# Long convolution and SwiGLU kernel: preceding block joined by a quarter turn after the product, third kernel spectrum built late, down projection with w_down stationary

## The chip, the core and the metric

The kernel runs on one core of one Trainium2 chip. A core has a matrix engine (PE, with its weight loads shown apart as PEld), a vector engine (DVE), an activation engine (ACT), a slower vector engine that also issues transfers (POOL), and a queue processor (SP) that only issues transfers. The metric is device time of one execution in microseconds: the median of 3 runs, 322.61 us before the change (322.45 to 322.96).

## What is computed

All tensors are bf16; the sequence has 2048 rows of 640 channels, the FFN is 1728 wide. `x` is `A_q`.

```python
def _A_ref(q, k, v, shift_k, ssm_k, ssm_D):       # q is layernorm(x)
    k_shift = sum over 4 taps t of k_pad[:, t:t+S] * shift_k[:, 3-t]
    kv = k_shift * v
    y = irfft(rfft(pad(kv)) * rfft(pad(ssm_k)))[:S]    # causal convolution, 2048 taps
    y = y + kv * ssm_D
    return q * y
def _B_ref(x, w_gate, w_up, w_down):
    return (silu(x @ w_gate) * (x @ w_up)) @ w_down
h = x + _A_ref(layernorm(x), A_k, A_v, A_shift_k, A_ssm_k, A_ssm_D)
h2 = h + _B_ref(layernorm(h), B_w_gate, B_w_up, B_w_down)
```

## The kernel before

The sequence is cut into 4 blocks of 512 rows (`NB = 4`, `MBLK = 512`). The convolution is done by blocks in a spectrum of odd frequencies: block `i` of `kv` becomes a spectrum X_i by matmuls with the constant `cs_t` (`x_transform`, L675); kernel block `p` becomes G_p by matmuls with `gb_t` (`g_transform0` L564, `g_transform` L612); products of X and kernel spectra are summed over pairs of blocks and brought back by matmuls with `ci_t` (`back`, L752). A spectrum is held as two "lanes" e = 0, 1 of 3 x 2 x 640 columns (two parts and a third, their half sum or sum, for complex products with three multiplications); one lane of 128 partitions has 0.98 MB.

A convolution of length 512 in this spectrum wraps: what runs over the block end comes back turned. The kernel before therefore joins each kernel block with the one ahead of it, once: `h_build` (L629 to L641) adds the neighbouring spectrum, turned by a quarter (parts swapped, one sign changed), to give H_p for p = 3, 2, 1. H_p goes to DRAM (`hd`) and comes back as lanes when a block needs it; X_i goes to DRAM (`xd`) likewise. `g_transform` for p = 1 to 3 works on folded kernel blocks (`g_fold`, L584 and L588: sum and difference of a block with its mirror image), which needs 4 or 6 matmuls a tile in place of 8; in the 6, two (L615) have a single row of `twos1` as weights. The time domain kernel blocks have time on the free axis, and are turned by DMA transposes (L542, L598).

Stages, by tag: C0 to C3 are the convolutions of the blocks, F0 to F3 the FFNs. A convolution stage: `shift` (taps on DVE, L653, L658, L659), `x_transform`, products (L937, L941 with earlier blocks; L955, L956 with H0; L895 in C0), `back` (L724, L732, L735 on DVE; L752 on PE; L410 on ACT; L758, L759 on DVE; `ln_stats` of h on ACT L700, L702, POOL L714), then the normed h (L767, called hn here) is turned by DMA transposes (L771) into `hlnT`. In F: gate and up projections (L831, 135 matmuls of 512 columns a block, weights streamed through 3 `wgu` buffers), silu and copy on ACT (L835, L836), product on DVE (L838), down projection with the activations `tT` as weights and `w_down` streaming (L856, 112 matmuls of 320 columns a block), with the residual h added on PE by an identity matmul (L852, 8 a block), copied out on ACT (L861).

No order is written by hand. Each piece of work is an `Op` with an engine, a duration, buffers and a priority; `Plan.schedule` walks a clock for each engine and picks, by priority and table offsets (`DELTA`, by tag, engine and function), which piece goes next. Buffers come from classes (`klass`) with a fixed number of slots, handed out first come first served. What comes out is one fixed order on each engine; SP issues its transfers strictly in that order, and one that must wait holds back all behind it.

The 4 PSUM tiles `ps` are shared by all matmul groups: PE fills one, ACT or DVE empties it, and only then is it free for another. `A_shift_k` is spread over partitions by 8 matmuls with `ones1` as weights at the very start (L511).

Of the kernel before, what the change touches and what calls it, by code (L numbers as in the profile page):

```python
# [54 lines left out]
    "C2 ACT back": 994,
    "C2 ACT evac": -900,
    "C2 ACT ln_stats": 97,
    "C2 DVE ln_stats": -1143,
    "C2 DVE shift": -33,
    "C2 DVE x_transform": -1000,  # L60
    "C2 PE x_transform": 30,
    "C2 SP k": 273,
    "C3 ACT evac": -103,
    "C3 ACT ln_stats": -100,
    "C3 DVE back": -1000,
    "C3 DVE ile_sequential_preLN__ssm_conv_h3__swiglu_ffn__prompt_kernel": -3,
    "C3 DVE ln_stats": -33,
    "C3 PE x_transform": -30,
    "C3 SP back": 200,
    "C3 SP k": 200,  # L70
    "C3 SP ldX": -1133,
    "C3 SP v": -1027,
    "C3 SP x": -30,
    "F0 PE ffn": 2872,
    "F0 POOL o": 200,
    "F0 SP w": 30,
    "F1 ACT ffn": 73,
    "F1 POOL o": 300,
    "F2 POOL o": -327,
    "F2 SP w": 100,  # L80
    "F3 DVE ffn": 30,
    "F3 SP w": 1030,
    "G ACT evac": 1662,
}
OPT = (True, (0, 1, 2, 3), (0,), (0, 1, 2, 3))
# [6 lines left out]
def make_consts():  # L92
# [24 lines left out]
    for n, (b, odd) in enumerate(((me, True), (pe, False), (po, True), (mo, False))):  # L117
        full = np.concatenate([np.full((HALF, 1), 2.0 * odd), (-1.0) ** odd * b[:, :0:-1], b], 1)
        for tt in range(NS):
            gb[:, tt, n, :] = full[:, tt * P:(tt + 1) * P].T  # L120
# [33 lines left out]
class Op:  # L154
    __slots__ = ("i", "eng", "dur", "fn", "deps", "succ", "allocs", "frees", "pri", "nwait", "ready", "soft", "alts", "key", "start", "end", "tag", "nbytes")


class Plan:
# [25 lines left out]
    def op(self, eng, dur, fn, r=(), w=(), pri=None, nbytes=0, alloc=(), alt=(), name=None):  # L184
        o = Op()
        o.i, o.eng, o.dur, o.fn, o.nbytes = len(self.ops), eng, dur, fn, nbytes
        o.alts = [(eng, dur, fn)] + list(alt)
        o.pri = self.pri if pri is None else pri
# [16 lines left out]
    def schedule(self):  # L205
# [37 lines left out]
        while done < len(ops):  # L243
# [40 lines left out]
            if o.nbytes:  # L284
                fly = flight[o.eng != "POOL"]
                s = max(st + o.dur + self.DMA_FIX, dma_free)
# [33 lines left out]
def kernel(  # L320
# [48 lines left out]
    NLANE, NWK, NS25, NWG = 7, 6, 3, 3  # L369
    klass("lane", NLANE, (P, 3, 2, D))  # L370
    klass("wk", NWK, (P, NS, D))
    klass("s25", NS25, (P, 2, D))
    klass("o", 2, (P, 2, D))
# [87 lines left out]
    taprows = [B("o", f"taps{k}") for k in range(2)]  # L461

    class Row:


        def __init__(self, k):
            self.b, self.k, self.dep = taprows[k // 2], k % 2, (taprows[k // 2], 1 << (k % 2))

        @property
        def t(self):  # L470
            return self.b.t[0:1, self.k, :]

# [17 lines left out]
    HB = 990  # L490


    def setup():
# [7 lines left out]
        with pl.at(-9.2):  # L501
            dma(lambda: ident.t[:], lambda: id_h.ap(), 32 * KB, w=[ident], q="ACT")
            pl.op("ACT", 0.46, lambda: nc.scalar.dma_start(out=skip.t, in_=A_ssm_D.rearrange("(o d) -> o d", o=1)), w=[skip.dep], nbytes=8 * KB, name="skip")
        for b, v in ((ones1, 1.0), (twos1, 2.0), (mhalf, -0.5)):
            dve(0.08, lambda b=b, v=v: nc.vector.memset(b.t[:], v), [], [b])
# [34 lines left out]
    def g_load0():  # L540
# [8 lines left out]
    def g_transform0(gT):  # L549

        def row():
            return gv(gT)[0:1, 0, :]
        dve(0.41, lambda: nc.vector.tensor_add(tap[0].t, skip.t, row()), [gT, skip.dep], [tap[0].dep])
        dve(0.41, lambda: nc.vector.tensor_sub(tap[1].t, skip.t, row()), [gT, skip.dep], [tap[1].dep])
        for b in (1, 3, 0, 2):
            tp = tap[1 - b % 2]
            for c in range(2):
                ps = B("ps")

                def mm(ps=ps, b=b, c=c, tp=tp):  # L560
                    for h in range(2):
                        hs = slice(h * NH, (h + 1) * NH)
                        for tt in range(NS):
                            nc.tensor.matmul(ps.t[:, h, 0:NH], gb_t.t[:, tt, b, c * P:(c + 1) * P], gv(gT)[:, tt, hs],  # L564
                                             start=(tt == 0), stop=False)
                        nc.tensor.matmul(ps.t[:, h, 0:NH], ones1.t[:], tp.t[:, hs], start=False, stop=True)  # L566
                pe(10 * c_mm(320), mm, [(gb_t, 2 - b % 2), gT, ones1, tp.dep], [ps])
                evac_lane(ps, H0, b, c)

    def g_fold(p):  # L570


        gst = B("h", f"gst{p}")

        def g():
            return flat(gst.t[:]).rearrange("p (c t) -> p c t", c=NDC)
        dma(g, lambda: A_ssm_k[:, p * MBLK:(p + 1) * MBLK].rearrange("(c p) t -> p c t", p=P), FULL, w=[gst])
# [5 lines left out]
        def sums():  # L583
            nc.vector.tensor_add(v()[:, :, 0], g()[:, :, HALF:MBLK], g()[:, :, HALF:0:-1])  # L584
            nc.vector.tensor_copy(v()[:, :, 0, 0:1], g()[:, :, HALF:HALF + 1])

        def diffs():
            nc.vector.tensor_sub(v()[:, :, 1], g()[:, :, HALF:MBLK], g()[:, :, HALF:0:-1])  # L588
            if p == 1:
                nc.vector.tensor_copy(s0c[p].t[:], g()[:, :, 0:1])  # L590
            else:
                nc.vector.tensor_add(s0c[p].t[:], s0c[p - 1].t[:], g()[:, :, 0:1])
            nc.vector.tensor_copy(v()[:, :, 1, 0:1], s0c[p].t[:])
        dve(c_tt(2 * D) + 0.25, sums, [gst], [(gf, 1)])
        dve(c_tt(2 * D) + 0.4, diffs, [gst] + ([s0c[p - 1]] if p > 1 else []), [(gf, 2), s0c[p]])
        gT = B("wgu", f"gT{p}")
        for dc in range(NDC):
            pl.op("SP", 1.25, lambda dc=dc: nc.sync.dma_start_transpose(out=gv(gT)[:, :, dc * P:(dc + 1) * P], in_=v()[:, dc].rearrange("p n t -> p (n t)")),  # L598
                  [gf], [(gT, 1 << dc)], nbytes=256 * KB, name="gT")
        return gT  # L600

    def g_transform(p, gT, dst):
        for b in (1, 3, 0, 2):
            e, n = b // 2, 1 - b % 2
            for c in range(2):
                ps = B("ps")

                def mm(ps=ps, b=b, c=c, n=n):
                    for h in range(2):
                        hs = slice(h * NH, (h + 1) * NH)  # L610
                        for tt in range(2):
                            nc.tensor.matmul(ps.t[:, h, 0:NH], gb_t.t[:, 2 + tt, b, c * P:(c + 1) * P], gv(gT)[:, 2 * n + tt, hs],  # L612
                                             start=(tt == 0), stop=(tt == 1 and n == 0))
                        if n:
                            nc.tensor.matmul(ps.t[:, h, 0:NH], twos1.t[:], gv(gT)[0:1, 2, hs], start=False, stop=True)  # L615
                pe((6 if n else 4) * c_mm(320), mm, [gb_t, gT] + ([twos1] if n else []), [ps], alloc=[dst[e].b])
                evac_lane(ps, dst, b, c)

    def g_sum_dve():
        for e in range(2):  # L620
            dve(c_tt(2 * D), lambda e=e: nc.vector.tensor_add(H0[e].t[:, 2], H0[e].t[:, 0], H0[e].t[:, 1]), [H0[e](15)], [H0[e](48)])
# [251 lines left out]
    with pl.at(-9):  # L873
        gT0 = g_load0()
# [123 lines left out]
```

## Time and profile before

| | us |
|---|---|
| median of 3 runs | 322.61 |
| the profiled execution's own time | 322.3 |
| its span, first to last instruction | 320.5 |
| PE busy | 283.2 (88%) |
| DVE busy | 222.6 (69%) |
| ACT busy | 192.7 (60%) |
| POOL busy | 32.2 (10%) |
| DMA moved | 67.52 MB, 211 GB/s mean |

The span is cut into stages below. A line of the timeline gives the start, how long the merged row lasts, engine, source line, operation, what is written from what, how often, and in brackets how long the engine stood idle ahead of it and what ended that. A row of groups gives count, then busy time and the mean duration of one in ns.

### The profile page before, as it was taken

The page shows a single profiled execution, that of the slowest core. Times are in us where ns is not written, and L with a number is a line of the kernel's source. Part 1 is how long each engine was busy: PE and PEld are TensorE (multiplying, and loading weights), DVE is VectorE, ACT ScalarE, POOL GpSimd, SP SyncE. Part 2 cuts the span into 40 slices and gives each one's busy share as a digit, 9 for nine tenths or more (in the row PEclk, how much of TensorE's full clock was granted, in tenths as well). Part 3 has the DMA queues.
Part 4 walks back from the last instruction along what each step waited for, and adds up shares of the span by engine and source line. Part 5 has one row for each costly group of instructions (what it writes and reads, how often), then busy time and mean ns, then how long its engine had stood idle before and what let it go on. Part 6 is the DMA issues. An engine that isn't in the chain of part 4 may idle for free.

```text
span 320.5 us, 4107 instructions
## 1 busy us (share of the span) xinstructions
PE 283.2 (88%) x1484; PEld 143.2 (45%) x1484; DVE 222.6 (69%) x284; ACT 192.7 (60%) x359; POOL 32.2 (10%) x34
## 2 busy tenths in 40 slices
PE   1499949983998859989989999999999999999993
PEld 0133622450254315555534545665444665444662
DVE  2992399479677999999999999986999730222100
ACT  1121895879399942594689768155995573445310
POOL 0000003003011140023002001300011020000000
PEclk9999995897599959999999999999999999999998
DMA  8998049436959999999965999999656224560011
GB/s 164 285 361 264 2 82 352 120 89 171 244 209 338 399 418 265 398 390 187 334 223 166 351 272 353 198 338 399 154 111 170 63 49 117 152 154 2 0 41 41
DMA packets 75911, 67.52 MB, mean 211 GB/s; under 512 B 33842, under 2 KB 70259, under 8 KB 75381
## 3 DMA queue, kind: packets, MB, share of 16 engines
q1 hardware_dynamic: 73662, 54.77, 59.0%
q0 software_dynamic: 2080, 12.45, 10.0%
q8 instruction: 11, 0.18, 0.2%
q10 hardware_dynamic: 150, 0.04, 0.1%
q14 instruction: 8, 0.07, 0.1%
HBM read 49.56 MB, written 12.45 MB: 193 GB/s over the span
## 4 chain that ended last, share of the span: by engine, by line
PE 25%; issue 22%; DVE 18%; ACT 17%; DMA 10%; SPq 3%; POOL 3%; POOLq 0%; DVEq 0%; ACTq 0%
PE ps L831 5%; PE ps L612 5%; DMA wgu<-in_B_w_gate_dram 5%; PE ps L564 4%; ACT junk L700 4%; ACT junk L702 3%; DVE lane L937 3%; PE ps L752 3%; DMA lane<-xd 3%; POOL mv L714 3%; PE ps L615 2%; PE ps L675 2%; DVE wk L653 2%; SPq L542 2%; ACT sg L835 2%
## 5 line engine op out<-in xcount | busy, mean ns | idle before, releaser
L831 PE MATMUL ps<-hlnT,wgu 128*128 128x512 bf16 x540 | 122.6, 384 | 8.4 <-DMA wgu<-in_B_w_gate_dram 4.8
L831 PEld LDWEIGHTS <-wgu 128*128 128x128 bf16 x540 | 53.0, 99 | 75.4 <-issue 11.0
L835 ACT ACTIVATE sg<-ps 128x512 bf16<-128x512 f32 (+1 forms) x56 | 33.5, 599 | 38.2 <-PE ps L831 36.0
L856 PE MATMUL ps<-wdA,tT 128*128 128x320 bf16 x384 | 55.6, 299 | 0.0
L856 PEld LDWEIGHTS <-tT 128*128 128x128 bf16 (+1 forms) x448 | 42.2, 98 | 20.6 <-issue 4.8
L838 DVE TENSOR_TENSOR tT<-sg,uc 128x512 bf16<-128x512 bf16 (+1 forms) x56 | 23.3, 420 | 35.7 <-ACT uc L836 35.4
L714 POOL TENSOR_TENSOR mv<-mv,mhalf 128x2 f32<-128x2 f32 (+1 forms) x12 | 21.9, 1827 | 183.2 <-DVE mv L712 183.2
L836 ACT CAST uc<-ps 128x512 bf16<-128x512 f32 (+1 forms) x56 | 32.8, 585 | 2.1 <-DVE tT L838 1.3
L861 ACT CAST o<-ps 128x640 bf16<-128x640 f32 x16 | 11.0, 691 | 35.1 <-PE ps L856 35.1
L612 PE MATMUL ps<-wgu,gb_t 128*128 128x320 bf16 x96 | 23.1, 370 | 10.0 <-ACT wdA L408 5.0
L937 DVE TENSOR_TENSOR lane<-lane,lane 128x3840 bf16<-128x3840 bf16 x12 | 25.8, 2154 | 4.5 <-DMA lane<-xd 4.5
L653 DVE TENSOR_TENSOR wk<-krun,w 128x2560 bf16<-128x2560 bf16 (+1 forms) x20 | 23.8, 1215 | 0.0
L408 ACT CAST lane<-ps 128x640 bf16<-128x640 f32 x31 | 20.0, 708 | 5.0 <-PE ps L615 4.5
L675 PE MATMUL ps<-wk,cs_t 128*128 128x320 bf16 x128 | 21.5, 332 | 0.8 <-ACT wdA L408 0.8
L564 PE MATMUL ps<-wgu,gb_t 128*128 128x320 bf16 x64 | 17.8, 425 | 4.4 <-DMA gb_t<-const_gb 4.4
L658 DVE TENSOR_TENSOR wk<-wk,wk 128x2560 bf16<-128x2560 bf16 (+1 forms) x15 | 18.1, 1213 | 0.0
L410 ACT ACTIVATE s<-ps,mv 128x640 bf16<-128x640 f32 x16 | 12.7, 795 | 7.8 <-PE ps L752 5.4
L675 PEld LDWEIGHTS <-cs_t 128*128 128x128 bf16 x128 | 13.5, 107 | 8.7 <-issue 1.6
L612 PEld LDWEIGHTS <-gb_t 128*128 128x128 bf16 x96 | 8.5, 107 | 18.4 <-issue 14.4
L408 ACT CAST h<-ps 128x640 bf16<-128x640 f32 x7 | 4.9, 699 | 19.0 <-PE ps L566 19.0
L752 PEld LDWEIGHTS <-ci_t 128*128 128x128 bf16 x128 | 12.4, 98 | 6.3 <-issue 1.0
L738 ACT ACTIVATE h<-wk,mv 128x640 bf16<-128x640 bf16 x16 | 13.4, 839 | 0.0
(83 smaller groups left out, 314.2 us busy)
## 6 DMA issues: line engine op xcount, KB each, us to landing
lane<-hd SPq DMA_DIRECT2D x10, 960.0 KB, 7.4
wgu<-in_B_w_gate_dram SPq DMA_DIRECT2D x24, 320.0 KB, 4.7
wgu<-in_B_w_up_dram SPq DMA_DIRECT2D x24, 320.0 KB, 4.4
lane<-xd SPq DMA_DIRECT2D x6, 960.0 KB, 7.4
xd<-lane POOLq DMA_DIRECT2D x4, 960.0 KB, 8.6
hd<-lane POOLq DMA_DIRECT2D x4, 960.0 KB, 9.1
krun<-in_A_k_dram SPq DMA_DIRECT2D x3, 1120.0 KB, 8.2
wk<-in_A_v_dram SPq DMA_DIRECT2D x4, 640.0 KB, 6.5
```

The source lines that it names most:

```text
L408: nc.scalar.copy(dst(), src())
L564: nc.tensor.matmul(ps.t[:, h, 0:NH], gb_t.t[:, tt, b, c * P:(c + 1) * P], gv(gT)[:, tt, hs], start=(tt == 0), stop=False)
L612: nc.tensor.matmul(ps.t[:, h, 0:NH], gb_t.t[:, 2 + tt, b, c * P:(c + 1) * P], gv(gT)[:, 2 * n + tt, hs], start=(tt == 0), stop=(tt == 1 an ...
L653: nc.vector.tensor_mul(dst.t[:, sl, :], ks, w4.t[:, j:j + 1, :].broadcast_to([P, n, D]))
L675: nc.tensor.matmul(ps.t[:, h, 0:NH], cs_t.t[:, s, n, c * P:(c + 1) * P], kv.t[:, s, h * NH:(h + 1) * NH], start=(a == 0), stop=(a == 1))
L714: pl.op("POOL", 1.4, lambda: nc.gpsimd.tensor_tensor(c(NS), c(2 * NS), mhalf.t[:, 0:len(slots)], op=ALU.pow), [(mv, bits << 8), mhalf], [( ...
L831: nc.tensor.matmul(ps.t[:, k, :], wg.t[:, kt, off:off + P], hT.t[:, kt, :], start=(kt == 0), stop=(kt == NDC - 1))
L835: act(c_act(MBLK) + 0.02, lambda ps=ps, sg=sg, np_=np_: nc.scalar.activation(sg.t[0:np_, :], ps.t[0:np_, 0, :], ACT.Silu), [(ps, 1)], [sg])
L836: act(c_act(MBLK), lambda ps=ps, uc=uc, np_=np_, lo=up_lo, k=len(offs) - 1: nc.scalar.copy(uc.t[0:np_, :], ps.t[lo:lo + np_, k, :]), [(ps, ...
L838: dve(c_tt(MBLK), lambda sg=sg, uc=uc, c=c, np_=np_: nc.vector.tensor_mul(tv()[0:np_, c, :], sg.t[0:np_, :], uc.t[0:np_, :]), [sg, uc], [( ...
L856: nc.tensor.matmul(ps.t[:, hh, 0:NH], tv()[0:np_, c, m * P:(m + 1) * P], wdc(c)[0:np_, hh * NH:(hh + 1) * NH], start=(c == 0 and not oadd) ...
L937: dve(c_tt(6 * D), lambda xl=xl, hl=hl: nc.vector.tensor_mul(xl.t[:], xl.t[:], hl.t[:]), [xl(), hl()], [xl()])
```

## The change

It has three named parts and several that come with them.

1. **Quarter turn after the product.** `h_build` is gone. The kernel spectra G_p are used as they are (their third part by `g_sum`). In `back`, the two combinations of the lanes (now buffers of a new class `eo`, r = 0 the sum, r = 1 the difference) of the block before are kept, and the new block's are added to them with parts swapped and one sign changed (L703 of the changed kernel). So block i needs only X_j times G_(i-j), and the neighbour comes from the kept `eo`.
2. **Third spectrum late.** G_3 is built in C3 (`g_block(3)`) and not at the start; it never goes to DRAM. G_1 and G_2 go to DRAM, and are used straight from their lanes when their block first needs them.
3. **Down projection turned** (`DSWAP`, blocks 0 to 2): w_down is the weight operand, `tT` streams; 5 x 14 matmuls of 512 columns a block (L803). The result is channel-major (`yT`, in a `wgu` buffer), is turned back by 5 DMA transposes a block (L514), and the residual is added on DVE (L811). Block 3 keeps the old form, with the residual on PE.
4. Only kernel block 3 is folded (`FOLD = (3,)`); blocks 1 and 2 take 8 matmuls a tile, none with a single row. Block 0 is loaded plainly and turned by 20 PE transposes (L525), not by a DMA transpose; its tiles still have one single-row matmul (`skip`) behind each 4.
5. Buffers: lanes 7 to 6, `wk` 6 to 5, `s25` 3 to 2, the two `o` halves become one whole, `eo` 3 new. Products with H0 in C1 and C2 are done in thirds (L931, L932). `DELTA` is a new table.

```diff
-OPT = (True, (0, 1, 2, 3), (0,), (0, 1, 2, 3))
+OPT = (True, (3,), (0,), (3,), (0, 1, 2))
...
-    NLANE, NWK, NS25, NWG = 7, 6, 3, 3
+    NLANE, NWK, NEO, NS25, NWG = 6, 5, 3, 2, 3
...
-        pl.op("SP", 2.5, lambda: nc.sync.dma_start_transpose(out=gv(gT), in_=A_ssm_k[:, 0:MBLK]), [], [gT], nbytes=FULL, name="gT")
+                        nc.tensor.transpose(pt[:, tt, dc * P:(dc + 1) * P], gsv(gst)[:, dc, (2 * a + tt) * P:(2 * a + tt + 1) * P], ident.t[:])
...
+                        if fold:
+                            ks = [(gb_t.t[:, 2 + tt, b, cs], gv(gT)[:, 2 * (1 - b % 2) + tt, hs]) for tt in range(2)]
...
+                        else:
+                            ks = [(gb_t.t[:, tt, b, cs], gv(gT)[:, tt, hs]) for tt in range(NS)]
+                            if p == 0:
+                                ks.append((ones1.t[:], skip.t[0:1, 0, hs]))
...
-            def f(e=e):
-                nc.vector.tensor_add(hp[e].t[:, 0], hp[e].t[:, 0], hm[e].t[:, 1])
-            def g(e=e):
-                nc.vector.tensor_sub(hp[e].t[:, 1], hp[e].t[:, 1], hm[e].t[:, 0])
...
+            old = before[r]
+            if old is not None:
+                for n in range(2):
+                    m = 3 << (2 * n)
+                    dve(c_tt(2 * D), lambda n=n, x=x, old=old, v=v: getattr(nc.vector, ("tensor_sub", "tensor_add")[n])(v(old)[:, 1 - n], v(x)[:, n], v(old)[:, 1 - n]),
+                        [(x, m), (old, 15 - m)], [(old, 15 - m)])
+            src.append((x, (0, 1)) if old is None else (old, (1, 0)))
+            before[r] = x
...
+        if i in DSWAP:
+            yT = B("wgu", f"yT{i}")
+            o = B("o", f"o{i}")
...
+                                nc.tensor.matmul(ps.t[:, 0, :], wdc(c)[0:np_, dc * P:(dc + 1) * P], tv()[0:np_, c, :], start=(c == 0), stop=(c == 13))
...
+                    tr_dma(lambda dc=dc: o.t[:, :, dc * P:(dc + 1) * P], lambda dc=dc: yT.t[:, dc, :], [(yT, 1 << dc)], [(o, 1 << dc)], alloc=[o], name="yT")
```

6. On SP at the start, the transfer of `gb_t` (the constant of the kernel spectra) has moved behind v, `cs_t`, `ci_t` and two pieces of w_down, and no transpose stands ahead of any of them any more.

**The order, place one: PE at the first X transform.** In the kernel before (`wgu_88` is the turned kernel block 0, `o_84` holds the single rows, `wk_75` is the kv of block 0) six tiles of kernel spectrum 0 stand ahead of it and two behind:

```order
L564 LDWEIGHTS gb_t
L564 MATMUL ps_65<-wgu_88,gb_t 128x320
L566 LDWEIGHTS ones_113
L566 MATMUL ps_65<-o_84,ones_113 128x320
L675 LDWEIGHTS cs_t
L675 MATMUL ps_66<-wk_75,cs_t 128x320
```

Changed (`wgu_87` is the turned kernel block 0, `wk_74` the kv):

```order
L582 LDWEIGHTS gb_t
L582 MATMUL ps_65<-wgu_87,gb_t 128x320
L582 LDWEIGHTS ones_108
L582 MATMUL ps_65<-o_83,ones_108 128x320
L638 LDWEIGHTS cs_t
L638 MATMUL ps_66<-wk_74,cs_t 128x320
```

The rows read alike; what moved is that here one tile stands ahead and seven behind.

**Place two: SP in C3.** Before (`xd`, `hd` are X and kernel lanes in DRAM, `hlnT` is the turned hn of block 2, `wk_75` is x):

```order
L771 DMA_TRANSPOSE hlnT_95<-s_0_80 128x5x128 x2
L430 DMA lane_67<-xd_120 128x3840
L430 DMA lane_70<-hd_126 128x3840
L430 DMA lane_68<-xd_122 128x3840
L430 DMA lane_72<-hd_124 128x3840
L430 DMA wk_75<-in_A_q_dram 128x2560
```

Changed (`wgu_88` holds yT of block 1 in the transposes, and weights in the last row):

```order
L409 DMA lane_72<-xd_114 128x3840
L514 DMA_TRANSPOSE hlnT_94<-s_0_81 128x5x128 x2
L409 DMA lane_71<-hd_120 128x3840
L514 DMA_TRANSPOSE o_83<-wgu_88 128x4x128 x2
L409 DMA lane_70<-xd_116 128x3840
L409 DMA lane_69<-hd_118 128x3840
L409 DMA wgu_88<-in_B_w_gate_dram 128x5x256
```

The transposes of o have come between the lane loads; eight lanes are loaded in C3 where ten were, with 6 slots for lanes in place of 7, and slots 71 and 72 are filled again as soon as a product has emptied them.

**Place three: DVE at the end of C3.** Before (`wk_74` and `lane_69` are what `back` reads):

```order
L956 TENSOR_TENSOR lane_67<-lane_67,lane_71 128x3840
L838 TENSOR_TENSOR tT_91<-sg_96,uc_98 128x512
L724 TENSOR_TENSOR lane_67<-lane_67 128x2560
L732 TENSOR_TENSOR wk_74<-lane_69,lane_67 128x1280 x2
L735 TENSOR_TENSOR lane_69<-lane_69,lane_67 128x1280 x2
```

Changed (`eo_79` is what r = 0 reads, `eo_80` what r = 1 reads):

```order
L698 TENSOR_TENSOR eo_78<-lane_67,lane_72 128x1280 x2
L703 TENSOR_TENSOR eo_79<-eo_78,eo_79 128x1280 x2
L791 TENSOR_TENSOR tT_90<-sg_95,uc_98 128x512
L698 TENSOR_TENSOR eo_78<-lane_67,lane_72 128x1280 x2
L703 TENSOR_TENSOR eo_80<-eo_78,eo_80 128x1280 x2
```

Four instructions stand where two did for each r: the turned sums have come into the last block's chain.

More of the change, by code (lines that the diff above doesn't have):

```diff
@@ L67 @@
[L67 to L83, printed above, removed]
+    "C0 ACT back": 3601,
+    "C0 ACT evac": -1548,
+    "C0 ACT g_sum": 1997,
+    "C0 DVE g_sum": -3262,
@@ L547, in evac_lane, with g_fold @@
         evac(D, lambda: v2(dst[e].t[:, n, c, :]), lambda: r3(ps.t), [ps], [dst[e](1 << (2 * n + c))], EITHER_G)
[L549 to L577, printed above, removed]
+    def g_fold(p, gst):
         gf = B("wk", f"gf{p}")
@@ L605, in g_transform, with mm @@
             for c in range(2):
                 ps = B("ps")
-                def mm(ps=ps, b=b, c=c, n=n):
+                def mm(ps=ps, b=b, c=c):
+                    cs = slice(c * P, (c + 1) * P)
                     for h in range(2):
                         hs = slice(h * NH, (h + 1) * NH)
[L611 to L615, printed above, removed]
@@ new lines, in g_block @@
+    def g_block(p):
+        if p in FOLD and p - 1 not in FOLD:
+            pl.op("POOL", 0.5, lambda: nc.gpsimd.memset(gb_t.t[0:1, 2, 0::2, :], 1.0), [], [(gb_t, 1 << k) for k in range(2)], name="first")
+        pm[p] = [Lane(B("lane", f"H{p}{e}")) for e in range(2)]
+        gst = g_load(p)
+        gT = g_turn_dma(p, g_fold(p, gst) if p in FOLD else gst)
+        g_transform(p, gT, p in FOLD)
+        g_sum(p)
+        if p < NB - 1:
+            for e in range(2):
+                dma(lambda e=e: HDR[p, e].t[:], lambda e=e: pm[p][e].t[:], LANE_B, r=[pm[p][e]()], w=[HDR[p, e]], q="POOL")
```

300 lines of the change are left out of this document (149 added, 151 removed).

## The prediction

> **What bounds the kernel now.** I read the busy shares first, then the span cut into stages, then the timelines of DVE and PE where stages meet.
>
> ```profile
> PE 283.2 (88%) x1484; PEld 143.2 (45%) x1484; DVE 222.6 (69%) x284; ACT 192.7 (60%) x359; POOL 32.2 (10%) x34
> ...
> PEclk9999995897599959999999999999999999999998
> ```
>
> By shares PE is the bound. The stages say more (columns: length, then busy time and count of PE, PEld, DVE, ACT, POOL; granted clock, DMA share, GB/s):
>
> ```profile
> 0.00:13.40 13.40, 2.42 (x8) 0.91 (x8) 6.89 (x13) 2.67 (x3) 0.20 (x4) 1.00 0.93 197
> 13.40:35.00 21.60, 21.52 (x71) 7.97 (x72) 13.20 (x23) 5.38 (x8) 0.00 (x0) 1.00 0.87 276
> 35.00:77.00 42.00, 32.11 (x170) 15.67 (x169) 31.29 (x42) 34.95 (x66) 4.68 (x4) 0.87 0.48 142
> 77.00:98.00 21.00, 18.97 (x76) 7.62 (x76) 13.90 (x22) 14.41 (x22) 2.13 (x4) 0.70 0.78 236
> 98.00:204.40 106.40, 97.75 (x531) 51.19 (x531) 103.45 (x121) 75.15 (x150) 17.62 (x14) 0.97 0.95 306
> 204.40:268.90 64.50, 63.97 (x377) 35.59 (x374) 47.91 (x54) 41.59 (x82) 5.92 (x6) 1.00 0.63 185
> 268.90:320.50 51.60, 46.51 (x256) 24.29 (x255) 5.95 (x14) 18.60 (x33) 1.63 (x3) 0.98 0.25 67
> ```
>
> From 98 to 204 DVE is full (103.45 of 106.40) and PE is not (97.75). Up to 98 nothing is full for long: chains over PE, ACT and DVE, with the PE clock down. The last 51.6 are PE alone. Three rows cut the span where it can be added up: the end of hn of block 0, the end of what `back` of block 3 needs, and the start of F3.
>
> ```profile
> 79.40 0.80 DVE L767 TENSOR_SCALAR s<-h,mv 128x640 bf16<-128x640 bf16 x2
> ...
> 249.17 1.55 DVE L735 TENSOR_TENSOR lane<-lane,lane 128x1280 bf16<-128x1280 bf16 x2
> ...
> 268.91 29.31 PE L831 MATMUL ps<-hlnT,wgu 128*128 128x512 bf16 x135
> ```
>
> So the span is 80.2 (to hn0) + 170.5 (DVE's long stretch, to 250.7) + 18.2 (to F3) + 51.6 (F3) = 320.5. I work out the four terms for the changed kernel. The execution's own time, 322.3, is 1.8 above its span, and the median of the runs 0.3 above that.
>
> **Term 1, up to hn0.** PE at the start:
>
> ```profile
> 13.48 1.25 PE L564 MATMUL ps<-wgu,gb_t 128*128 128x320 bf16 x4 [4.44 <-DMA gb_t<-const_gb]
> ...
> 31.74 0.44 PE L566 MATMUL ps<-o,ones 1*128 1x320 bf16 x1
> 32.12 5.97 PE L675 MATMUL ps<-wk,cs_t 128*128 128x320 bf16 x32
> 37.94 0.70 PE L564 MATMUL ps<-wgu,gb_t 128*128 128x320 bf16 x4
> ...
> 41.23 0.30 PE L566 MATMUL ps<-o,ones 1*128 1x320 bf16 x1
> ...
> 77.07 0.69 PE L612 MATMUL ps<-wgu,gb_t 128*128 128x320 bf16 x2 [5.00 <-ACT wdA L408]
> ```
>
> From 13.48 to 32.12 twelve groups of five take 1.55 each. Behind the X transform four of them take 0.90 each (37.94 to 41.53). The granted clock reads 1.00 in both (0.00 to 35.00 above), yet the pace differs by 1.7; so that column does not show what held the start back. In this mixture with single-row matmuls the slow pace held 18.6 us, and it ended inside the X transform, which has none.
>
> The X transform needs kv, which DVE makes:
>
> ```profile
> 9.25 2.29 DVE L653 TENSOR_TENSOR wk<-krun,w 128x1280 bf16<-128x1280 bf16 x3
> ...
> 21.19 0.83 DVE L659 TENSOR_TENSOR wk<-wk,wk 128x1280 bf16<-128x1280 bf16 x1
> ```
>
> The two tap rows (0.8 us inside this stretch) are gone, and the half for r = 0 is done two instructions (1.5) before the end: the X transform, now second on PE, starts at 22.0 - 0.8 - 1.5 = 19.7, and not at 32.1. It takes 6 as before, warming PE: 25.7. The seven tiles left are 14 groups: 14 x 0.90 = 12.6, to 38.3, against 41.5. That `gb_t` lands later costs nothing: its 13.48 moves by a few us, and only one tile (3.1) waits for it ahead of 19.7.
>
> From there ACT leads:
>
> ```profile
> 36.58 2.50 ACT L408 CAST lane<-ps 128x640 bf16<-128x640 f32 x4
> 38.92 1.32 ACT L622 ACTIVATE h<-h 128x1280 bf16<-128x1280 bf16 x1
> ...
> 41.58 0.74 ACT L702 ACTIVATE junk<-wk 128x640 bf16<-128x640 bf16 x1
> ...
> 42.44 0.74 ACT L700 ACTIVATE junk<-wk 128x640 bf16<-128x640 bf16 x1
> ...
> 64.65 0.80 ACT L410 ACTIVATE s<-ps,mv 128x640 bf16<-128x640 f32 x1 [0.56 <-PE ps L752]
> ...
> L738 ACT ACTIVATE h<-wk,mv 128x640 bf16<-128x640 bf16 x16 | 13.4, 839 | 0.0
> ...
> L714 POOL TENSOR_TENSOR mv<-mv,mhalf 128x2 f32<-128x2 f32 x8 | 12.0, 1496 | 92.2 <-DVE mv L712 92.2
> ```
>
> A copy costs 0.6, a statistic 0.86 from start to start. After 38.3: last copy (39.5), two statistics (41.3), two scalings (43.9), then the changed order has 9 copies and 3 h rows ahead of the first result of `back` (9 x 0.6 + 3 x 0.84 = 7.9, to 51.8), four results with a scaling and a copy between (4 x 0.8 + 1.3 + 0.6 + about 0.9 of waiting for PE = 6, to 57.8), and 8 statistics (6.9, to 64.7). Then 0.4 of small sums, the first two hn (0.8), a product on DVE of 2.15 beside the power's 1.5, the last two hn (0.8) and about 1 of signals: **70.0**. Before, it took 38.7 from the end of G0; here 31.7, since `back` no longer stands behind single-row tiles at the slow pace and G3 is not built here at all (the 77.07 row is its wait). Term 1: 80.2 to 70.0.
>
> **Term 2, DVE to the end of block 3's products.** The idle time in the old 170.5:
>
> ```profile
> L838 DVE TENSOR_TENSOR tT<-sg,uc 128x512 bf16<-128x512 bf16 (+1 forms) x28 | 11.6, 419 | 4.8 <-ACT uc L836 4.5
> ...
> 214.02 2.16 DVE L937 TENSOR_TENSOR lane<-lane,lane 128x3840 bf16<-128x3840 bf16 x1 [1.20 <-DMA lane<-xd]
> 219.50 2.16 DVE L937 TENSOR_TENSOR lane<-lane,lane 128x3840 bf16<-128x3840 bf16 x1 [3.32 <-DMA lane<-xd]
> ```
>
> 4.8 between 98 and 204, 4.5 for lanes, 6.5 ahead of 98 (21.0 less 13.9, a little of it before hn0), 0.6 besides: 16.4, so 154.1 of work. Removed after hn0: `h_build`, 18 instructions of 1280 (0.75 each by L735's pair) and 2 scalings, 14.5; one tap product and two lane products that now come earlier (1.4 + 4.2). Added ahead of block 3's end: 12 quarter-turn sums (9.0), four sums of the last `ps` of 1280 and two scalings (4.0), the fold of block 3 (1.9), 4 residual sums (3.0), and 1.4 since the thirds (24 x 0.75) take more than 8 whole ones (2.08 each); 0.9 less by products of F2 that move behind the end. That is -20.1 + 19.3 - 0.9 = -1.7: **the quarter turn saves DVE nothing**, it moves the work. Idle time in the new order: DVE reaches X1's sums about 5 after hn0, while ACT has six copies of G2, a scaling and eight copies of X1 behind 64.7 (14 x 0.6 + 1.3, to 74.4), and PE, idle for some 4 ahead of them, begins them slowly as at 77.07 (2.5): 77, a wait of 3. FFN products: 5 as now. Residual sums waiting for five transposes: 1. Lanes:
>
> ```profile
> L430 SPq DMA_DIRECT2D lane<-hd x10: 319/338/558, 126.3 to 212.8; - x10
> L430 SPq DMA_DIRECT2D lane<-xd x6: 319/369/796, 127.3 to 210.7; - x6
> ...
> DMA to landing us min/median/max: 5.2/7.4/10.5
> ```
>
> With 6 slots, slot 72 is refilled once its product is done and is needed 5.6 of DVE work later, slot 71 3.7 later, slot 70 4.7 later. Landing at 5.2 gives waits of 0, 1.5 and 0.5, at 7.4 they are 2, 3.7 and 2.7, at 10.5 about 17 in all with the others. I take 5, between the first two, since two reloads can overlap. Sum: 154.1 - 1.7 + 14 = **166.4**.
>
> **Terms 3 and 4.** From the last DVE input, PE needs `back` for r = 1 (2.3) and the down projection that is left, 63 matmuls of 512 columns at 29.31/135 = 0.217: 2.3 + 13.7 = 16.0, plus 0.1 of signalling. hn3 and its transposes take about as long: 262.78 + 0.80 - 251.78 = 11.8 from `back` to hn3 before, some 1 less now as r = 0 is further ahead, then a second transpose (1.2) and a landing (3.1).
>
> ```profile
> 251.78 2.33 PE L752 MATMUL ps<-lane,ci_t 128*128 128x320 bf16 x16
> ...
> 262.78 0.80 DVE L767 TENSOR_SCALAR s<-h,mv 128x640 bf16<-128x640 bf16 x2 [0.88 <-POOL mv L714]
> ...
> 311.42 3.42 PE L856 MATMUL ps<-wdA,tT 128*128 128x320 bf16 x24
> 314.68 0.81 PE L856 MATMUL ps<-wdB,tT 128*128 128x320 bf16 x4
> ...
> L771 SPq DMA_TRANSPOSE hlnT<-s x16: 1200/1227/2444, 77.8 to 264.5; - x16
> ...
> DMA to landing us min/median/max: 2.6/3.1/7.0
> ```
>
> Term 3: **16.1**. F3 is unchanged in form: **51.6**. As to PE, a narrow matmul costs (314.68 - 311.42)/24 = 0.136, so the turned down projection saves 120 x 0.136 - 70 x 0.217 = 1.1 a block, and G3 adds 32 x 0.136 = 4.4: its work from F0 on is the same within 1. F0 starts near 77 and waits some 3.5 for the first silu; up to `back` of block 3 stand three gate and up projections (88), 2.1 down projections (32) and 7 transforms of 32 (24), with some 4 of gaps: 228.5, 8 before DVE's 236.4. So what PE saves is covered by DVE, and where PE falls more than 8 behind, that cover is gone (rival 3).
>
> Sum: 70.0 + 166.4 + 16.1 + 51.6 = 304.1, with 1.8 and 0.3: **306**.
>
> **Rivals.**
> 1. *The single-row mixture cools PE again.* Seven tiles then cost 3.10 and not 1.80: 7 x 1.30 = 9.1, and everything behind shifts: 315. For it: the mixture never warmed PE in 18.6 us. Against: it ran warm for 3.6 us here, and rows that start cold (77.07) follow an idle gap of 5. The Trainium skill ("TensorE: Matmul & The Clock Gate", Part 1) says the gate opens after about 3.4 us of sustained activity and closes after an idle window; by it G0 stays warm, as I forecast. The row from 13.48 to 32.12 contradicts its first half, since activity without a gap stayed slow five such windows long. So: 14 in 100.
> 2. *Waits shrink.* Lanes land at 5.2, X1 is ready in time, ACT's chain is 3 shorter: 3 + 6 less, 297. 9 in 100.
> 3. *SP holds everything (slower than before).* In C3 the lane loads, the transposes of hn and o, and F2's weights stand in one SP order; o's transposes wait for PE's down projection, lanes behind them for the transposes, DVE for the lanes, FFN products for weights behind the lanes. If each load lands in 10.5, waits are 17 in place of 5 (+12), and the weights come late as they did once before:
>
> ```profile
> 116.15 6.60 PE L831 MATMUL ps<-hlnT,wgu 128*128 128x512 bf16 x20 [4.80 <-DMA wgu<-in_B_w_gate_dram]
> ```
>
> 4.8, and 2.3 for ten matmuls at the slow pace (6.60 less 20 x 0.217): +7. 306 + 19 = 325. It decides once PE is more than the 8 late. Against it: DMA moves two lanes less in C3. 10 in 100.
> 4. *Two half losses together*, 319 to 323: 7 in 100.
>
> **How the numbers follow.** Forecast 60 in 100 (301 to 312). The range reaches over rival 1 and most of rival 2: 298 to 319; outside are rival 3, rival 4 and a little below. A measurement of this kernel can tell 0.2% (0.65 us) from no change. Faster: 60 + 14 + 9 + 4 = 87; within 0.2%: 3; slower: 10.
>
> **What would show it.** Right: the X transform starts near 20, hn0 ends near 70, DVE is full from there with lane waits of some 5, `back` of block 3 gets its last input near 236, F3 takes 51.6. Wrong: G0's groups at 1.55 behind the X transform; PE, not DVE, the fuller engine from 80 to 230; SP waiting for o's transposes while DVE waits for lanes.

## The result and the profile after

The changed kernel takes 311.25 us (median of 4 runs, 309.74 to 314.09), the kernel before 322.78 (322.45 to 323.24): a ratio of 0.965, 95% interval [0.958, 0.973]. The forecast was 306. The profiled execution of the changed kernel took 310.19 with a span of 308.3, against a forecast span of 304.1. Comparisons leave disturbed runs out, so a ratio is not always the quotient of the medians beside it.

Busy shares and the granted clock of the changed kernel (share of the span in brackets, then instructions; below, the clock in 40 slices):

```profile
PE 267.4 (87%) x1394; PEld 134.5 (44%) x1394; DVE 224.5 (73%) x294; ACT 192.8 (63%) x362; POOL 28.2 (9%) x33
...
PEclk9999999979999999999999999899999999999999
```

PE is 16 us shorter in busy time. In the kernel before, the slices of 8.0 us with a low clock lay from 48 to 64 (5 and 8), from 72 to 88 (7 and 5) and at 112 (5), the last slice left aside; now there are two, a 7 at 62 and an 8 at 193 (slices of 7.7). The three rows that cut the span, now (start, us, engine, line):

```profile
67.92 0.79 DVE L737 TENSOR_SCALAR s<-h,mv 128x640 bf16<-128x640 bf16 x2
...
235.77 1.55 DVE L703 TENSOR_TENSOR eo<-eo,eo 128x1280 bf16<-128x1280 bf16 x2
...
256.24 29.38 PE L784 MATMUL ps<-hlnT,wgu 128*128 128x512 bf16 x135
```

| Term | before | forecast | measured |
|---|---|---|---|
| 1, to the end of hn of block 0 | 80.2 | 70.0 | 68.7 |
| 2, to the end of what block 3's `back` needs | 170.5 | 166.4 | 168.6 |
| 3, to F3 | 18.2 | 16.1 | 18.9 |
| 4, F3 | 51.6 | 51.6 | 52.1 |

All of the gain is in term 1: -11.5. The other three together are 0.7 shorter than before (239.6 after 240.3), where 6.2 was forecast.

PE at the start, timeline of the changed kernel:

```profile
18.04 1.25 PE L582 MATMUL ps<-wgu,gb_t 128*128 128x320 bf16 x4 [4.64 <-DMA gb_t<-const_gb]
...
21.15 5.80 PE L638 MATMUL ps<-wk,cs_t 128*128 128x320 bf16 x32
26.80 0.70 PE L582 MATMUL ps<-wgu,gb_t 128*128 128x320 bf16 x4
27.43 0.30 PE L582 MATMUL ps<-o,ones 1*128 1x320 bf16 x1
...
39.20 4.52 PE L582 MATMUL ps<-wgu,gb_t 128*128 128x320 bf16 x32
...
50.83 4.52 PE L723 MATMUL ps<-eo,ci_t 128*128 128x320 bf16 x32
```

The X transform starts at 21.15 (32.12 before), the 14 groups left of G0 take 12.40/14 = 0.886 each behind it, and `back` of block 0 starts at 50.83; before it started at 63.29.

Term 2 by windows (length, then busy time of PE, PEld, DVE, ACT, POOL), first the kernel before:

```profile
80.20:250.70 170.50, 159.36 (x845) 81.82 (x846) 155.93 (x175) 117.08 (x224) 22.84 (x19) 0.95 0.89 281
```

and the changed kernel:

```profile
68.70:237.30 168.60, 152.96 (x755) 72.95 (x753) 153.56 (x192) 116.89 (x227) 17.32 (x16) 0.99 0.82 233
```

DVE's work fell by 2.4, and its idle time rose from 14.6 to 15.0. The prediction named "PE, not DVE, the fuller engine from 80 to 230" as a sign of being wrong: there DVE was busy for 136.87 us and PE for 135.81, so it is nearly a draw. The two long waits, on DVE and then on PE, are new:

```profile
133.64 1.56 DVE L811 TENSOR_TENSOR o<-o,h 128x1280 bf16<-128x1280 bf16 x2 [4.47 <-DMA o<-wgu]
...
201.44 0.42 DVE L791 TENSOR_TENSOR tT<-sg,uc 128x512 bf16<-128x512 bf16 x1 [3.50 <-ACT uc L789]
```

```profile
196.78 10.49 PE L784 MATMUL ps<-hlnT,wgu 128*128 128x512 bf16 x40 [3.29 <-DMA hlnT<-s]
...
223.72 9.87 PE L784 MATMUL ps<-hlnT,wgu 128*128 128x512 bf16 x45 [2.19 <-ACT uc L789]
...
235.60 1.25 PE L723 MATMUL ps<-eo,ci_t 128*128 128x320 bf16 x8 [0.49 <-ACT uc L789]
237.78 3.42 PE L723 MATMUL ps<-eo,ci_t 128*128 128x320 bf16 x24 [0.93 <-ACT s L389]
```

The first is a residual sum of block 0 that waits for the transposes of the turned down projection. The second is the first product of F2, which is late because PE got block 2's transposed hn late. The 3.29 ahead of 196.78 is that wait.

### The profile page after: what moved, and what is told of

Read it like the earlier page. It is cut to its first block, busy times and chain, and to the rows that moved or that the text cites. A ratio compares the mean times of both kernels' runs of the same rounds, so it can differ in the third digit from the quotient of the medians.

```text
span 308.3 us, 3965 instructions
## 1 busy us (share of the span) xinstructions
PE 267.4 (87%) x1394; PEld 134.5 (44%) x1394; DVE 224.5 (73%) x294; ACT 192.8 (63%) x362; POOL 28.2 (9%) x33
## 3 DMA queue, kind: packets, MB, share of 16 engines
q0 software_dynamic: 1792, 10.49, 8.8%
HBM read 46.29 MB, written 10.49 MB: 184 GB/s over the span
## 5 line engine op out<-in xcount | busy, mean ns | idle before, releaser
L582 PE MATMUL ps<-wgu,gb_t 128*128 128x320 bf16 x224 | 36.9, 313 | 10.0 <-ACT lane L387 5.1
L803 PE MATMUL ps<-tT,wdA 128*128 128x512 bf16 x180 | 41.9, 379 | 3.3 <-ACT wgu L806 1.8
L677 POOL TENSOR_TENSOR mv<-mv,mhalf 128x2 f32<-128x2 f32 (+1 forms) x12 | 18.5, 1542 | 149.8 <-DVE mv L675 115.7
L582 PEld LDWEIGHTS <-gb_t 128*128 128x128 bf16 x224 | 21.3, 101 | 22.3 <-issue 6.7
L387 ACT CAST lane<-ps 128x640 bf16<-128x640 f32 x39 | 24.8, 722 | 4.0 <-PE ps L582 3.2
L803 PEld LDWEIGHTS <-wdA 128*128 128x128 bf16 x180 | 16.8, 98 | 23.8 <-issue 6.0
L723 PE MATMUL ps<-eo,ci_t 128*128 128x320 bf16 x128 | 18.6, 299 | 1.6 <-ACT s L389 0.9
L806 ACT CAST wgu<-ps 128x512 bf16<-128x512 f32 x15 | 8.4, 581 | 12.1 <-PE ps L803 9.4
L830 PE MATMUL ps<-wdA,tT 128*128 128x320 bf16 x96 | 13.7, 299 | 0.0
L663 ACT ACTIVATE junk<-wk 128x640 bf16<-128x640 bf16 x16 | 11.8, 739 | 1.9 <-DMA wk<-in_A_q_dram 1.7
```

The lines of the kernel that those rows point to most:

```text
L387: nc.scalar.copy(dst(), src())
L582: nc.tensor.matmul(ps.t[:, h, 0:NH], wt, mv, start=(k == 0), stop=(k == len(ks) - 1))
L677: pl.op("POOL", 1.4, lambda: nc.gpsimd.tensor_tensor(c(NS), c(2 * NS), mhalf.t[:, 0:len(slots)], op=ALU.pow), [(mv, bits << 8), mhalf], [( ...
L723: nc.tensor.matmul(ps.t[:, hh, 0:NH], ci_t.t[:, c, 1 - n, s, :], x.t[:, 2 * pos[n] + c, hh * NH:(hh + 1) * NH], start=(k == 0), stop=(k == 3))
L803: nc.tensor.matmul(ps.t[:, 0, :], wdc(c)[0:np_, dc * P:(dc + 1) * P], tv()[0:np_, c, :], start=(c == 0), stop=(c == 13))
```

## The experiments

In all of them the planned order is taken as it is and then edited, so that nothing else moves. Each names what it moves by stage, engine, kind and occurrence.

**What is the start worth, and what holds PE slow?** `later` puts operations behind a named one, with all that depend on them, and deals out the PSUM tiles anew.

```
+ x = 8 tiles of C0 x_transform, their casts, their 6 sums
+ order = later(order, x + [first tile of G1], last cast of G0)
```

> The X transform of block 0 (eight tiles, with their casts and the sums behind them) stands behind all eight tiles of G0 on PE; the rest in the order of the changed kernel. Theory M (the mixture with single-row matmuls keeps PE at its slow pace when it starts cold): 16 groups of five at 1.55 from 18.0 to 42.8, then X slowly at first to 48.5, and hn0 some 9 to 12 later than 68.7; time 320 to 324, the whole gain of the change gone. Rival T (the slow pace ends by itself some 3 to 5 us after matmuls start, single rows or not): G0 from 18.0 to about 34, X warm to 39, hn0 at 69 to 72; time 311 to 315.

Measured: 329.66 us, ratio to before 1.020 [1.015, 1.026].

```
- if p == 0:
-     ks.append((ones1.t[:], skip.t[0:1, 0, hs]))
```

> As x_behind_g0, and G0's 16 single-row matmuls are left out, so the skip term is missing in the output. Theory M: with no single rows in it G0 is slow for 3 us only (10 matmuls of 0.31), then its other 54 take 0.14 each: G0 from 18.0 to about 29, X to 33.5. If the slow pace has another cause (the time since the start of the program, or the weights changing with each matmul), G0's matmuls stay at 0.31 up to about 23 or longer, and G0 ends at 32 or, at 0.31 all along, at 38.

Measured: 322.76 us, ratio 1.008 [0.998, 1.018]. The timelines of PE, then the end of hn on DVE, with single rows:

```profile
17.71 1.25 PE L583 MATMUL ps<-wgu,gb_t 128*128 128x320 bf16 x4 [4.56 <-DMA gb_t<-const_gb]
18.89 0.44 PE L583 MATMUL ps<-o,ones 1*128 1x320 bf16 x1
...
42.56 6.52 PE L639 MATMUL ps<-wk,cs_t 128*128 128x320 bf16 x32
...
63.87 7.19 PE L583 MATMUL ps<-wgu,gb_t 128*128 128x320 bf16 x40 [10.44 <-ACT lane L388]
...
87.99 0.79 DVE L738 TENSOR_SCALAR s<-h,mv 128x640 bf16<-128x640 bf16 x2
```

and without them:

```profile
17.48 9.72 PE L581 MATMUL ps<-wgu,gb_t 128*128 128x320 bf16 x56 [4.52 <-DMA gb_t<-const_gb]
...
52.51 7.09 PE L581 MATMUL ps<-wgu,gb_t 128*128 128x320 bf16 x40 [10.44 <-ACT lane L388]
...
76.53 0.79 DVE L736 TENSOR_SCALAR s<-h,mv 128x640 bf16<-128x640 bf16 x2
```

Theory M holds. With the rows, 80 matmuls without a gap stayed at the slow pace for 24.85 us, all 16 groups at 1.55. Without them 56 took 9.72: from start to start the first fifteen stand 0.27 apart (4.0 us in all, where ten and 3 us were expected) and the rest 0.14. Why the rows do this stays open. The loss was larger than forecast (hn ends 20 later, not 9 to 12; 329.66 us, not 320 to 324), and the row with 10.44 says why: that wait is the same with and without rows. ACT shows what it is, here with the rows:

```profile
61.97 1.27 ACT L591 ACTIVATE h<-h 128x1280 bf16<-128x1280 bf16 x1 [9.36 <-DVE h L590]
```

A scaling on ACT waits for a sum on DVE, which stands there behind X's sums and block 1's taps; casts stand behind the scaling, and PE behind the casts. In the changed kernel's order DVE does this work while G0's tail runs. So the early X transform gives two things: PE gets warm in it, and DVE gets work beside G0. What is won at hn does not all reach the end: without the rows hn ends 11.5 earlier (77.3 after 88.8), and the time is 6.9 shorter by medians.

**What is the folded form of G1 and G2 worth?** In the kernel before, the single-row matmuls of the three later spectra are left out.

```
- if n:
-     nc.tensor.matmul(ps, twos1, gT row, start=False, stop=True)
```

> The kernel before without the single-row matmuls of G1, G2 and G3 (so their odd spectra lack the middle tap's part); all else as before. Theory (the folded form of G1 and G2 in the first stage, with a single-row matmul in every second tile, keeps PE slow from 48.2 to 63.3 and holds block 0's back transform, whose data are there at 57.4): back starts near 58 and not at 63.3, hn of block 0 ends near 75 and not at 80.2, and the time falls by 3 to 5, to 318 to 320. Rival (casts on ACT and DVE hold these tiles, not PE's pace): hn of block 0 moves by 1 or less, the time by 1 or less.

Measured: 318.79 us, ratio 0.986 [0.981, 0.991].

```profile
47.80 7.00 PE L612 MATMUL ps<-wgu,gb_t 128*128 128x320 bf16 x36 [0.97 <-ACT lane L408]
...
56.47 1.25 PE L750 MATMUL ps<-wk,ci_t 128*128 128x320 bf16 x8
...
73.38 0.80 DVE L765 TENSOR_SCALAR s<-h,mv 128x640 bf16<-128x640 bf16 x2
```

`back` starts 6.8 earlier and hn ends at 74.2, 6.0 earlier. That is over half of term 1's 11.5, and most of it reaches the end: 3.8 by the spans of the two profiled executions, 4.9 by medians. Another 2.3 of the 11.5 is G0's earlier end (39.2 after 41.5). No run here separates what gave the remaining 3.

**Early or late third spectrum?** All of G3's work is left out, once of the kernel before and once of the changed one.

```
+ G3's load, fold, transposes, tiles, casts: fn = lambda: None
+ (before) its final form from G2; (changed) its product reads X twice
```

> The kernel before without the building of G3 in the first stage (load, fold, transposes, tiles with their single rows, casts); the sums for its final form read G2 in its place, as many as before, so block 3's output is another. This is the price of building it early. If, as the prediction said, the tiles of G3 are part of the 38.7 us from the end of G0 to hn of block 0, hn ends 3 or more earlier than 80.2. If they stand wholly behind that chain (their casts follow the statistics of h on ACT), hn stays within 1 of 80.2, F0's first matmul comes 8 to 12 earlier than 92.7, and the time falls by no more than DVE's idle time between hn and 98, so by 3 to 6.

> The changed kernel without any of G3's work in block 3's stage (its load, fold, five transposes, 32 matmuls, 8 casts and the sums of its thirds); the product with G3 reads X twice, so the output of block 3 is another. This is the price of building the third spectrum late. On DVE 4 us (2.0 for the fold, 2.1 for sums), on PE 4.6, on SP 7.4, on ACT 5. Theory (DVE bounds the kernel up to hn of block 2): F2 starts 3 to 5 earlier than in the changed kernel and the time falls by 3 to 5. Rival (what it takes lies beside waits): less than 1.5.

Measured: 320.78 us (0.993 [0.989, 0.997]) for the kernel before, 311.35 (0.963 [0.958, 0.967]) for the changed one, whose own runs in that call gave 310.80 (0.960 [0.955, 0.965]). In the kernel before:

```profile
79.07 0.80 DVE L767 TENSOR_SCALAR s<-h,mv 128x640 bf16<-128x640 bf16 x2
...
81.33 6.63 PE L675 MATMUL ps<-wk,cs_t 128*128 128x320 bf16 x32 [12.71 <-DVE wk L659]
...
88.31 4.48 PE L831 MATMUL ps<-hlnT,wgu 128*128 128x512 bf16 x20 [0.35 <-ACT lane L408]
```

hn still ends at 79.9, so G3 had no part in term 1; F0 starts only 4.4 earlier, since X1 then waits 12.7 for kv of block 1. Built early it cost 2.7 us; built late it costs nothing that can be measured. In the changed kernel without it F2 still starts where it did:

```profile
191.31 2.16 DVE L907 TENSOR_TENSOR lane<-lane,lane 128x3840 bf16<-128x3840 bf16 x1 [2.65 <-DMA lane<-hd]
...
196.72 10.49 PE L784 MATMUL ps<-hlnT,wgu 128*128 128x512 bf16 x40 [3.62 <-DMA hlnT<-s]
```

My theory here (3 to 5) fell. DVE was spared some 4, yet its last sum for `back` ends at 237.3 as before. The wait for a lane grew from 1.93 to 2.65 and the one for hn's transposes from 3.29 to 3.62, and this execution was already 1.1 behind at hn of block 1; what took the rest is not resolved.

**Is DVE the bound in term 2?** The 12 quarter-turn sums do nothing.

```
- getattr(nc.vector, ("tensor_sub", "tensor_add")[n])(old, x, old)
+ None
```

> Leaves out the 12 quarter-turn sums (L703), so the outputs of blocks 1 to 3 are joined without what they should take from each other; order and all else as in the changed kernel. 12 x 0.74 = 8.9 us of DVE. Theory (DVE full from hn0 on): DVE's end of block 3's products comes 6 to 9 us earlier (228 to 231; the part that is missing was covered by waits for transposes and lanes that stay where they are), and the time falls to 302 to 305 us. Rival (PE is the bound, at 87% of the span): only block 3's four sums are on the path to its back transform, 3.0 us; the time falls by 3 or less, to 308 or more.

Measured: 307.83 us (0.952 [0.946, 0.957]), 3.4 less than the changed kernel, between the two theories. DVE's last input of `back` and PE's second half of it:

```profile
230.04 1.55 DVE L698 TENSOR_TENSOR eo<-lane,lane 128x1280 bf16<-128x1280 bf16 x2
```

```profile
236.03 3.42 PE L722 MATMUL ps<-eo,ci_t 128*128 128x320 bf16 x24 [0.93 <-ACT s L389]
```

DVE ends at 231.6, 5.7 earlier; PE comes only 1.75 earlier and is now the later one. So DVE bounds term 2 with PE right behind it, not 8 behind.

**Do o's transposes on SP cost what the wait of 4.47 says?**

```
+ move([two residual sums of F0, their stores], behind 4th of C2's last products)
```

> Block 0's two residual sums (L811) stand four products and sums later on DVE, everything else as in the changed kernel. In the changed kernel DVE waited 4.47 us for them (until 133.64) while the last casts of the X tiles that the next sums (L648) read ended by about 130.3. Theory (DVE is what bounds the kernel from hn0 to block 3's products): DVE starts L648 near 130.3, so DVE's end of block 3's products moves from 237.3 to about 234, and the time falls by about 3.3 to some 308 us; a little less if the sums then wait themselves, or if lanes come late behind. Rival (PE or SP sets the pace there): the wait only moves to the next product of F1, DVE's end stays at 237, and the time stays within 0.5 us of the changed kernel's 311.

```
+ move([load of x of block 2], behind 4th transpose of hn of block 1)
```

> As osum_later, and the load of x of block 2 is issued on SP ahead of the last four transposes of block 0's o (they took SP from 125.4 to 130.6, and ACT then waited 1.75 us for x, with F1's second cast queued behind). Theory (o's transposes on SP are what makes F1's first products late): x lands near 130, F1's first product, which waited 2.51 in osum_later, does not wait, DVE is 3 to 4 earlier from 137 on than in the changed kernel, and the time falls by 1 to 3 (308 to 310), the rest lost again to lanes and to F2's start, which stay where DMA puts them. Rival (PE's gate and up projection sets F1's first products): the wait stays over 1.5 and the time at 311 to 312.

Measured: 312.17 us (0.967 [0.962, 0.972]) for osum_later and 310.26 (0.960 [0.954, 0.966]) for x2_sooner_osum. The sums alone gained nothing (the rival's forecast): the first product of F1 waits in their place, here in osum_later:

```profile
136.83 0.43 DVE L791 TENSOR_TENSOR tT<-sg,uc 128x512 bf16<-128x512 bf16 x1 [2.51 <-ACT uc L789]
```

The changed kernel shows where it comes from, SP first, then ACT:

```profile
125.42 5.15 SPq L514 DMA_TRANSPOSE o<-wgu  x4
130.62 0.57 SPq L409 DMA_DIRECT2D wk<-in_A_q_dram  x1
```

```profile
135.02 0.74 ACT L663 ACTIVATE junk<-wk 128x640 bf16<-128x640 bf16 x1 [1.75 <-DMA wk<-in_A_q_dram]
...
135.76 0.56 ACT L789 CAST uc<-ps 128x512 bf16<-128x512 f32 x1
```

Four transposes hold SP for 5.15, the load of x stands behind them, ACT waits for x, and F1's cast stands behind that. With the load ahead of the transposes the product waits 0.70:

```profile
135.41 0.43 DVE L791 TENSOR_TENSOR tT<-sg,uc 128x512 bf16<-128x512 bf16 x1 [0.70 <-ACT uc L789]
```

So this wait of 2.5 is shown to come from SP's order. The time fell just short of the theory (308 to 310); what the wait is worth, about 1, is not separated from the changed kernel's runs.

**What makes F2 late?**

```
+ move([load of X of block 0, half 1], behind 4th transpose of hn of block 2)
```

> One load of block 3's lanes (960 KB, X of block 0, second half) is issued on SP behind the last two transposes of hn of block 2 and not ahead of them; all else as in the changed kernel, where F2's first matmul waited 3.29 us for these transposes (196.78) and its first 40 matmuls took 10.49 in place of 8.8. Theory (PE is the bound from F2's start to the end, DMA traffic ahead of the transposes makes F2 late): F2 starts 2 to 3 us earlier, the wait before it falls under 1.5, the slow matmuls behind it are gone (1.7), and the time falls by 3 to 4, to 307 to 308 us. Rival (DVE is the bound up to block 3's products): the lane product at 195.78 now waits some 2 us, the products end at 237 as before, and the time stays at 311, or rises by up to 2.

> The moves of hT2_first and x2_sooner_osum together. If DVE bounds the stretch up to hn of block 2 and PE the one from F2's start, the gains add: 4 to 7 us under the changed kernel, 304 to 307. If only one of the two engines bounds both, one of the gains is missing: 308 or more.

```
+ move([last 3 statistics of x of block 3], behind the casts of X3's first tiles)
+ move([products 3 and 4 of F2], one and two large products earlier)
```

> three_moves, and three moves more: three of the eight statistics of x of block 3 stand behind the two casts for which F2's first matmul waited 2.44 us on ACT, and two products of F2 stand one and two large products earlier on DVE, so that PE does not wait 2.2 us near 221. Theory (PE bounds the kernel from F2's start to block 3's back transform, with DVE's products only just behind it): both waits fall under 1.5, the slow matmuls behind them (1.7 each) go, back of block 3 starts up to 2.5 earlier, where DVE's products (235.5) then hold it; time 1.5 to 3 under three_moves, 4 to 6 under the changed kernel of the same call. Rival (DVE alone bounds this stretch): DVE's end of products stays at 235 to 236 and the time within 1 of three_moves, 309.

> The changed kernel once more, as the measure for the runs beside it. Its four runs so far lie between 309.7 and 314.1. If the spread comes from PE, which after some of its waits of about 2 us runs slowly for 3 us and after others does not, runs fall again within 309 to 314, and the slower ones show a lower granted clock; the median lies between 311 and 312.

Measured: 311.42 us (0.964 [0.957, 0.971]) for hT2_first, 308.90 (0.956 [0.950, 0.961]) for three_moves, 308.95 (0.955 [0.951, 0.959]) for six_moves and, for the changed kernel beside the last, 310.80 (0.960 [0.955, 0.965]; 308.44 to 313.89). That is a little lower than was expected of it (median 311 to 312, runs from 309); its slowest run does show the lowest clock, 0.968. In hT2_first the transposes no longer hold F2; ACT's casts, which stand behind eight statistics, do:

```profile
196.99 9.05 PE L784 MATMUL ps<-hlnT,wgu 128*128 128x512 bf16 x39 [2.44 <-ACT wk L387]
```

One wait took the place of the other: the time stayed (rival). In three_moves the gains do not add to 304 to 307 either; with 308.90 one of them is missing. In six_moves the wait at F2's start is 1.55 and F2 starts 3.3 earlier than in the changed kernel, but DVE's end moves by only 0.3, and PE waits twice, through ACT's casts, for products on DVE:

```profile
205.42 4.14 PE L638 MATMUL ps<-wk,cs_t 128*128 128x320 bf16 x16 [2.27 <-ACT uc L789]
...
224.91 9.40 PE L784 MATMUL ps<-hlnT,wgu 128*128 128x512 bf16 x35 [2.40 <-ACT uc L789]
...
235.45 1.56 DVE L703 TENSOR_TENSOR eo<-eo,eo 128x1280 bf16<-128x1280 bf16 x2
```

The theory that PE bounds the kernel from F2's start on fell. three_moves and six_moves have medians some 2 us under the changed one, but the intervals overlap; whether they are faster is open.

## Why the prediction came out as it did

The direction held, and so did the mechanism of term 1 but for the part that it gave to G3; 4.2 of span were missed: -1.3 in term 1, +2.2 in term 2, +2.8 in term 3, +0.5 in term 4.

1. *X transform first, PE warm behind it* (19.7, then 14 groups of 0.90): 21.15 and 0.886. Right, and rival 1 is refuted: the mixture ran warm for 12.4 us. That `gb_t` lands later was said to cost nothing; kv was ready at 20.56 and the tile of G0 ahead ended at 21.15, so it cost 0.6. x_behind_g0 shows that the mixture alone did not warm PE in 24.85 us. The Trainium skill ("TensorE: Matmul & The Clock Gate", Part 1) has about 3.4 us of sustained activity open the gate; 24.85 us of matmuls with single rows among them did not, and 9.72 without the rows did, so for this mixture the measurement contradicts it.
2. *31.7 from G0's end to hn*: 29.5. The sum over ACT came out row by row: the first result of `back` stood at 51.8 in it and the end of the eight statistics at 64.7, and they came at 52.17 and 64.76:

```profile
52.17 0.79 ACT L389 ACTIVATE s<-ps,mv 128x640 bf16<-128x640 f32 x1 [0.68 <-PE ps L723]
...
64.57 0.19 ACT L665 ACTIVATION_READ_ACCUMULATOR junk<-h 128x1 f32 x1
```

The reason given for the gain was right as to the single-row tiles ahead of `back` (before_no_rows: 6.0) and wrong as to G3: "the 77.07 row is its wait" does not belong to this chain (before_no_g3: hn within 0.4). The sum did not rest on it.

3. *DVE's work in term 2, -1.7*: -2.4. Right: the quarter turn moves DVE's work and saves almost none.
4. *DVE's idle time, 16.4 to 14*: 14.6 to 15.0 by the windows. The old idle time was read 1.8 too high: a wait of 4.13 that ends at 98.02 was counted twice, in the 4.8 "between 98 and 204" and in the 6.5 "ahead of 98", while some 2.3 of small waits were left out:

```profile
98.02 0.43 DVE L838 TENSOR_TENSOR tT<-sg,uc 128x512 bf16<-128x512 bf16 x1 [4.13 <-ACT uc L836]
```

So the work was 155.9 and not 154.1, and of the 2.2 that term 2 missed, 1.2 is work (153.6 where 152.4 was forecast). The other 1.0 is idle time, and there the step that failed is "Residual sums waiting for five transposes: 1": they waited 4.5. Lanes, forecast at 5, waited 1.9, X1's sums some 1.9 in place of 3, and FFN products 4.6, forecast at 5. Rival 3's mechanism, transposes, lanes and loads in one SP order, was at work at a small size (x2_sooner_osum).
5. *PE is 8 ahead of DVE at `back` of block 3*: 235.60 against 237.3, under 2. F2's wait of 3.29, the slow matmuls behind it (10.49 for 40, where 45 took 9.87 at the fast pace: 1.7) and the wait of 2.19 used up the cover. So term 3 had 24 matmuls of `back` left and not 16, and waits of ACT's casts: 0.9 more of `back`, 0.9 of item 6 and 1.0 of waits are its 2.8.
6. *Down projection at 0.217 a matmul*: its groups of 14 stand 3.23 apart, 0.231 each:

```profile
242.74 2.76 PE L803 MATMUL ps<-tT,wdA 128*128 128x512 bf16 x12
245.34 0.70 PE L803 MATMUL ps<-tT,wdB 128*128 128x512 bf16 x2
245.97 2.76 PE L803 MATMUL ps<-tT,wdA 128*128 128x512 bf16 x12
```

The two matmuls with `wdB` take 0.63 of it from start to start (245.34 to 245.97), the twelve ahead of them 0.217 each. So 63 of them cost 0.9 more than forecast. The old form's groups of 30 have the same step, 0.75 for the four with `wdB`, so that a group takes 4.28 (260.34 to 264.62):

```profile
260.34 0.45 PE L852 MATMUL ps<-h,ident 128*128 128x320 bf16 x2
260.62 3.42 PE L856 MATMUL ps<-wdA,tT 128*128 128x320 bf16 x24
263.88 0.81 PE L856 MATMUL ps<-wdB,tT 128*128 128x320 bf16 x4
264.62 0.45 PE L852 MATMUL ps<-h,ident 128*128 128x320 bf16 x2
```

Five groups of 3.23 make 16.2 a block, four of 4.28 make 17.1: the turned form saves 1.0 a block on PE, near the forecast of 1.1, though both prices a matmul were too low. The two forms were not run against each other in one order, so what this is worth in time is not shown.

7. *0.3 from execution to median*: 1.1. The changed kernel's four runs beside the four of the kernel before spread over 4.4 us, those over 0.8; in later calls the kernel before spread over 3.3 to 8.1 too. The profile of a run of the changed kernel of 313.89 shows where its 3.8 of span lie: F2 starts at 199.18 after a wait of 4.90, and 45 later matmuls take 11.56 where the shown execution has 9.87.

That the time follows term 1 within some 4 us is the firmest reading. hn of block 0 ends at 68.7, 74.2, 77.3, 80.2 and 88.8 in the changed kernel, before_no_rows, x_behind_g0_no_rows, the kernel before and x_behind_g0; from there to the end it is 239.6, 242.5, 243.6, 240.3 and 240.5.

## What to carry over

Look for the stage in which no engine is full, and order there by what gives the other engines work and what warms PE; the nearly full engines behind it passed most of the gain on here. Work taken off the fuller engine pays only up to the lead of the next one, so measure that lead at the point where the two meet. A new transpose on a queue is priced by what is issued behind it too, not by its own landing alone.

## Unexpected on the chip

A matmul of a single row in every group of five kept PE at the slow pace (1.55 us a group) for 24.85 us from a cold start, but did not cool it once warm (12.4 us at 0.886 a group). After waits of PE up to 2.07 us the matmuls of the changed kernel and its variants went on at the fast pace. After twelve waits of 2.19 to 2.44 they ran slowly ten times, for some 3 us and mostly at a cost of 1.7, and twice not (9.87 for 45 behind 2.19, 9.05 for 39 behind 2.44). After waits of 2.79 and more they ran slowly but for two (a wait of 3.09 in no_g3 and one of 3.42 in hT2_first). So one kernel can have runs on both sides of it: behind its wait of 2.19 the changed kernel took 9.87 in one execution and 11.56 in another.
